# The x^T of batch 1's last head pair by DMA transpose, with a new set of due times: an attention and feed-forward kernel on one core

## The chip, the cores and the metric

The kernel runs on one core of one Trainium2 chip. The metric is the device time of one execution in microseconds. The time before is the median of 8 runs. The profile is of one more execution; times inside it count from the start of its span.

## What is computed

Sorted attention over 4 batches, 8 heads, 768 tokens, 64 values a head, and then a feed-forward network with a squared ReLU. The essence of the reference:

```python
P = sort_net                                  # (4, 8, 8, 8)
for _ in range(5):
    P = exp(P - max(P, -1)); P /= sum(P, -1); P /= sum(P, -2)
k_sorted, v_sorted = P @ blocks of k, P @ blocks of v      # 8 blocks of 96 tokens
attn = softmax(q_block @ k_sorted_block.T / 8)             # block by block
x = (attn @ v_sorted_block) as (3072 tokens, 512)
h = maximum(x @ w_in, 0)                      # (3072, 2048)
out = h * h @ w_out                           # (3072, 512)
```

## The kernel before

**Units.** Attention is worked through in pairs of heads, written (batch, pair), with pairs 0 to 3 of each of the batches 0 to 3. The feed-forward part takes 384 tokens at a time: U0 to U7, two for a batch. Each has 16 up chunks (`up`, L988: four 128x384 matmuls over the four pairs' rows of xT, one for each kc) and three times four down chunks (`down`, L1023: four 128x512 matmuls). U2.5 is the sixth up chunk of U2; D1.2.3 is the last down chunk of the third token tile of U1. An up chunk takes 0.65 us of TensorE, a down chunk 0.863.

**The steps of a pair**, by the letter that stands in DUES (L21) and in this text:

- N and V (`s_nat`, L743): sorted k and v in their natural layout, two pairs at once, so N(2,1) gives pairs 2 and 3 of batch 2. 16 matmuls on 32x32 tiles (L759), then two evictions from PSUM, one for each pair, by ACT or DVE. V is then written to DRAM and read back in another layout by SP (`v_way`, L783 and L789).
- Z (`s_turn`, L810): k and q of one pair transposed by DMA on SP (L816, L839); DVE then splits q in two (L843, L844).
- S (`s_sc`, L643): the scores, two halves of four matmuls (L657), each followed by two exponentials on ACT (L697).
- A (`s_av`, L857): the two halves of the values (L873, 8 matmuls each), each followed by the normalisation on DVE, a reciprocal (L885) and a product (L886).
- X (`s_xt`, L905): x^T, the pair's 128 rows of the tile xT that the up chunks read. It goes one of two ways. Either TensorE transposes eight 96x128 blocks into PSUM (L928) and ACT or DVE copies them to xT (L935), or SP issues a DMA_TRANSPOSE (L910) that goes from SBUF to SBUF[...]. Before the change the second way is taken for batches 2 and 3, for pairs 0 to 2 of batch 1, and for the second half of pairs 0 to 2 of batch 0.
- T and K do for batch 0 what V and N do later; W builds weights of the sorting (`build_wt`, L477).

S halves, A halves, N and V evictions share two PSUM slots (`p2`, ring r2), taken by turns: a step waits until the step two before it in that ring has been read out.

**The order.** A planner in the kernel (`Plan.run`, L136) writes every engine's order by its own costs before anything runs. On TensorE it merges two queues: the attention steps, in the order of their due times, and the feed-forward chunks. A due time is a number of chunks: the step goes as soon as that many have gone and its inputs are there by the plan. Once written, the order of each engine is fixed, and so is that of the DMA issues on SP and POOL: an engine waits for its next instruction's inputs and does nothing else.

**Loads.** q, k and v of batches 2 and 3 are loaded by POOL, six DMAs of 384 KB for each batch (`load_late`, L1136). They overwrite buffers and would disturb other transfers, so a tiny copy on POOL (`hold`, L1138) waits for x^T of the batch before; for batch 2 it waits for pairs 0 to 2 of batch 1 and not for pair 3 (`HP - (b == 2)`, L1139 and L1142). The loads of batch 2 follow it on POOL at once.

The functions that the change touches:

Of the kernel before, what the change touches and what calls it, by code (L numbers as in the profile page):

```python
# [18 lines left out]


DUES = {  # L21
    (0, "K"): (-133.5, -48.0, -102.0, -78.0),
    (0, "S"): (-77.0, -37.5, -97.5, -40.0),
    (0, "T"): (-99.0, -11.5, -42.0, -63.5),
    (0, "A"): (-64.0, 16.0, -15.0, -31.5),
    (0, "X"): (-7.5, 41.5, -9.5, -18.5),
    (0, "W"): (-100.0,),
    (1, "V"): (20.5, 30.5),
    (1, "Q"): (32.0,),
    (1, "N"): (None, 36.0),  # L30
    (1, "Z"): (None, None, 38.0, 43.5),
    (1, "S"): (32.5, 40.5, 43.5, 50.0),
    (1, "A"): (41.0, 41.5, 48.5, 50.0),
    (1, "X"): (45.0, 41.5, 48.5, 55.0),
    (2, "L"): (58.0,),
    (2, "N"): (75.5, 70.5),
    (2, "V"): (63.0, 88.5),
    (2, "Z"): (84.0, 84.5, 90.5, 96.0),
    (2, "S"): (90.0, 96.5, 100.5, 102.0),
    (2, "A"): (95.0, 98.0, 104.0, 102.5),  # L40
    (2, "X"): (100.0, 101.5, 110.0, 104.0),
    (3, "L"): (110.5,),
    (3, "N"): (130.0, 137.5),
    (3, "V"): (117.0, 140.5),
    (3, "Z"): (134.5, 143.0, 154.5, 154.0),
    (3, "S"): (145.0, 150.5, 159.0, 155.0),
    (3, "A"): (148.0, 153.5, 162.5, 156.5),
    (3, "X"): (159.0, 248.0, 167.0, 326.0),
}


# [133 lines left out]
def kernel(  # L185
# [12 lines left out]
    B, H, S, D = q.shape  # L198
# [5 lines left out]
    HP = H // 2  # L204
# [35 lines left out]
    def cost_b(n):  # L240
        return (0.17 + 0.82e-3 * n, 0.15 + 0.53e-3 * n)

    def one_of(eng, cost, fn, deps):
        return plan.add(eng, cost if eng == AD else cost[AD.index(eng)], fn, deps)

    def copy(eng, out, in_):
        if eng == "ACT":
            nc.scalar.copy(out=out, in_=in_)  # L248
        else:
            nc.vector.tensor_copy(out=out, in_=in_)  # L250
# [653 lines left out]

    def s_xt(u, due=0, eng=AD, own=True):  # L905
        early = u.b == 0 and u.halves == (1,) and u.hp < HP - 1
        if early or u.b > 1 or u.b == 1 and u.hp < HP - 1:
            def turn(e):
                t0 = S * u.b + BLK * u.i0
                nc.sync.dma_start_transpose(  # L910
                    out=xT[:, u.hp, t0:t0 + BLK * u.ni].rearrange("p (n q) -> p n q", q=BLK),
                    in_=u.ao.rearrange("p n e d -> p (n e d)"))

            sp = plan.add("SP", 1.4, turn, u.norms)
            op = plan.add("WAY", 6.0 if early else 1.3, lambda e: None, [sp], tail=5.0 if early else None)
            rao.use(u.nao, op)
            for hf in u.halves:
                x_done[u.b, u.hp, hf] = op
            return
        st = {}  # L920

        ring = r1 if own else rf

        def mm(e):
            st["p"] = xtp = ((ps1 if own else psf)
                             .tile([128, u.ni, BLK], BF16, tag="p1" if own else "pf", name="xtp"))
            for n in range(u.ni):
                nc.tensor.transpose(  # L928
                    out=xtp[:, n, :],
                    in_=u.ao[:, n, :, :].rearrange("p e d -> p (e d)"),  # L930
                    identity=ident[0:96, 0:96])

        def ev(e):
            t0 = S * u.b + BLK * u.i0
            copy(e, xT[:, u.hp, t0:t0 + BLK * u.ni], st["p"].rearrange("p n q -> p (n q)"))  # L935

        s1, old = ring.take()
        pe = plan.add("PE", 0.342 if u.full else 0.17, mm, u.norms + old, due)
        op = one_of(eng, cost_b(BLK * u.ni), ev, [pe])
        ring.use(s1, pe, op)  # L940
        rao.use(u.nao, pe)
        for hf in u.halves:
            x_done[u.b, u.hp, hf] = op
# [138 lines left out]
    for name in FIRST.split():  # L1082
        stage, n = name[0], int(name[1])
        eng = "ACT" if stage.isupper() else "DVE"
        stage = stage.upper()
        if stage == "F":
            f_piece(n)
            continue
        if n not in us:
            us[n] = Unit(0, n, (0,))  # L1090
            us[n].q_op = qops[n]
        u = us[n]
        own = (name[2:] == "'") ^ (stage in "TX")
        if stage == "K":
            u.k_op = s_sort(u, 1, early=True, eng=eng, own=own)
        elif stage == "V":
            u.v_op = s_sort(u, 2, early=True, eng=eng, own=own)
        elif stage == "S":
            s_sc(u)
        elif stage == "T":  # L1100
            s_vt(u, eng=eng, own=own)
        elif stage == "A":
            s_av(u)
        else:
            s_xt(u, eng=eng, own=own)
# [6 lines left out]
              "T": lambda b, hp, due: s_vt(units[b, hp], due),  # L1112
              "A": lambda b, hp, due: s_av(units[b, hp], due),
              "X": lambda b, hp, due: s_xt(units[b, hp], due),
              "V": lambda b, g, due: s_nat(b, g, 2, due),
              "N": lambda b, g, due: s_nat(b, g, 1, due)}
# [83 lines left out]
```

The softmax here doesn't subtract the row's maximum and nothing guards it: scores larger than these inputs give would overflow.

## Time and profile before

| | us |
|---|---|
| median of 8 runs (218.43 to 218.96) | 218.66 |
| the profiled execution, its own time | 218.67 |
| its span, first to last instruction | 216.9 |
| TensorE busy | 211.4 |
| ACT busy | 120.5 |
| DVE busy | 110.0 |
| POOL busy | 30.4 |
| TensorE on up chunks (L997) | 87.8 |
| TensorE on down chunks (L1027) | 85.1 |
| X(1,3) on TensorE (L928, 8 transposes, at 74.66) | 0.34 |
| X(1,3)'s copy on DVE (L250) | 0.56 |

The time around the span (1.8 us) is the execution's time less its span. A line of the chain of work that ended last gives start, duration and what; there, a matmul's piece runs from end to end. A line of the timeline gives start, duration, engine, line, operation, output<-inputs and count, and in brackets the engine's idle time before it and what ended that. The DMA view names queue q0 for what POOL issues (software_dynamic) and q1 for what SP issues (hardware_dynamic), with packets, MB and the time that the packets took as a share of 16 engines.

### The profile page before, as it was taken

What the parts mean: (1) busy time and instruction counts of PE and PEld (TensorE: products, weight loads), DVE (VectorE), ACT (ScalarE), POOL (GpSimd) and SP (SyncE); (2) the same over time, 40 slices, a digit from 0 to 9 for tenths busy, and PEclk for the clock granted to TensorE, in tenths of its full rate; (3) what the DMA queues carried; (4) which work ended last, traced back from release to release, by engine and by line L of the source; (5) the groups of instructions that cost most, each with busy time, mean ns of one, the idle gap of its engine ahead of it and who ended that gap; (6) DMA issues with size and microseconds to landing.
All of it is one profiled execution on the core that took longest, in us unless ns stands there. A gap on an engine that the chain in (4) does not pass through costs nothing.

```text
span 216.9 us, 4928 instructions
## 1 busy us (share of the span) xinstructions
PE 211.4 (97%) x1958; PEld 120.0 (55%) x1958; DVE 110.0 (51%) x310; ACT 120.5 (56%) x246; POOL 30.4 (14%) x55
## 2 busy tenths in 40 slices
PE   8989999999999999999999999999999999999994
PEld 3566666446566565446675465446666465456543
DVE  6778748218785446505886055327676155005400
ACT  4665795227955277417884277238765276137521
POOL 7994222200000600000000420000000000000000
DMA  5999999999993599199982699559997310120012
GB/s 64 198 202 207 207 207 205 190 184 260 229 188 99 126 199 216 34 185 209 245 156 74 127 189 215 111 139 126 257 181 144 92 51 0 48 80 20 0 48 97
DMA packets 47831, 31.51 MB, mean 145 GB/s; under 512 B 27264, under 2 KB 42880, under 8 KB 47808
## 3 DMA queue, kind: packets, MB, share of 16 engines
q0 software_dynamic: 12736, 13.63, 39.1%
q1 hardware_dynamic: 35072, 17.56, 36.6%
q8 instruction: 15, 0.25, 0.4%
q14 instruction: 8, 0.07, 0.1%
HBM read 29.70 MB, written 8.72 MB: 177 GB/s over the span
## 4 chain that ended last, share of the span: by engine, by line
PE 91%; DVE 5%; ACT 1%; DMA 1%; issue 1%; DVEq 0%
PE hp L997 39%; PE op L1027 37%; PE p L873 4%; PE p L657 3%; PE p L759 2%; PE op L1055 2%; PE p L667 1%; PE vbp L723 1%; DVE p_sb L402 1%; PE p L624 1%; DMA p_sb<-in_sort_net_dram 1%; PE xtp L928 1%; DVE cs L400 1%; ACT p_sb L432 1%; DVE ao L886 1%
## 5 line engine op out<-in xcount | busy, mean ns | idle before, releaser
L997 PE MATMUL hp<-xT,w_in_bf 128*128 128x384 bf16 x506 | 87.8, 327 | 0.0
L1027 PE MATMUL op<-w_out_bf,h 128*128 128x512 bf16 x368 | 85.1, 379 | 0.0
L1008 DVE TENSOR_TENSOR h<-h 128x384 bf16<-128x384 bf16 x128 | 43.9, 355 | 57.3 <-ACT h L1005 56.9
L1005 ACT ACTIVATE h<-hp 128x384 bf16<-128x384 f32 x128 | 61.9, 494 | 18.2 <-PE hp L997 15.6
L997 PEld LDWEIGHTS <-w_in_bf 128*128 128x128 bf16 x506 | 47.7, 98 | 31.4 <-issue 0.9
L1027 PEld LDWEIGHTS <-h 128*128 128x128 bf16 x368 | 34.3, 98 | 37.0 <-issue 1.0
L248 ACT COPY ob<-op 128x512 f32<-128x512 f32 (+2 forms) x25 | 14.2, 568 | 51.6 <-PE op L1027 49.1
L886 DVE TENSOR_TENSOR ao<-p,rec 96x512 bf16<-96x512 f32 x32 | 22.0, 686 | 1.1
L697 ACT ACTIVATE et<-p 96x384 bf16<-96x384 f32 x40 | 16.8, 487 | 8.0 <-PE p L657 7.7
L873 PEld LDWEIGHTS <-et 96*128 96x128 bf16 x256 | 11.6, 97 | 5.0 <-issue 0.7
L885 DVE RECIPROCAL rec<-p 96x8 f32<-96x8 f32 x32 | 6.4, 200 | 10.5 <-PE p L873 8.7
L1139 POOL COPY held<-xT 1x3 bf16<-1x3 bf16 (+1 forms) x2 | 0.4, 182 | 78.6 <-DMA xT<-ao 78.6
L418 PE MATMUL p<-ones 128*128 128x512 bf16 (+1 forms) x30 | 9.4, 434 | 1.1 <-DVE ones L269 1.1
L657 PEld LDWEIGHTS <-kx 128*128 128x128 bf16 x80 | 8.4, 144 | 2.3 <-issue 0.2
L873 PE MATMUL p<-vblk,et 96*128 96x65 bf16 x192 | 9.5, 193 | 0.0
L657 PE MATMUL p<-qz,kx 128*128 128x192 bf16 x80 | 9.0, 246 | 0.0
L250 DVE CAST kn<-p 128x768 bf16<-128x768 f32 x5 | 4.8, 958 | 8.3 <-PE p L759 8.1
L250 DVE CAST vn<-p 128x768 bf16<-128x768 f32 x6 | 5.7, 956 | 5.8 <-PE p L759 4.4
L322 POOL DMA_DIRECT2D kb<-in_k_dram x10 | 6.4, 642 | 4.4 <-DMA w_in_bf<-in_moe_w_in_dram 2.0
L322 POOL DMA_DIRECT2D qb<-in_q_dram x8 | 6.2, 770 | 5.1 <-DMA w_in_bf<-in_moe_w_in_dram 2.2
L322 POOL DMA_DIRECT2D vb<-in_v_dram x10 | 6.3, 629 | 3.4 <-DMA w_in_bf<-in_moe_w_in_dram 3.4
L687 ACT ACTIVATE et<-p 96x768 bf16<-96x768 f32 x8 | 6.2, 803 | 0.3 <-PE p L667 0.2
(84 smaller groups left out, 123.1 us busy)
## 6 DMA issues: line engine op xcount, KB each, us to landing
out_dram<-ob SPq DMA_DIRECT2D x23, 256.0 KB, 2.3
qb<-in_q_dram POOLq DMA_DIRECT2D x8, 384.0 KB, 11.4
v_way<-vn SPq DMA_DIRECT2D x6, 396.0 KB, 5.3
vblk<-v_way SPq DMA_DIRECT2D x6, 396.0 KB, 4.2
vb<-in_v_dram POOLq DMA_DIRECT2D x6, 384.0 KB, 11.8
kb<-in_k_dram POOLq DMA_DIRECT2D x6, 384.0 KB, 10.8
w_in_bf<-in_moe_w_in_dram POOLq DMA_DIRECT2D x4, 512.0 KB, 11.8
w_out_bf<-in_moe_w_out_dram POOLq DMA_DIRECT2D x4, 512.0 KB, 17.8
```

Source lines behind the costliest of these rows:

```text
L248: nc.scalar.copy(out=out, in_=in_)
L250: nc.vector.tensor_copy(out=out, in_=in_)
L322: nc.gpsimd.dma_start(out=dst, in_=src)
L418: nc.tensor.matmul(out=p2[slot][:, 0, 0:128 * r].rearrange("p (r x) -> p r x", r=r), lhsT=ones, rhs=ones[:, None, :].to_broadcast([128, r, ...
L657: nc.tensor.matmul(out=scp[:, n // 2, 2 * BLK * (n % 2):2 * BLK * (n % 2 + 1)], lhsT=kx_r[u.kx][:, i::NB], rhs=qz_r[u.qz][:, :, :, C0 * i: ...
L697: nc.scalar.activation(out=et.rearrange("p h x -> p (h x)")[:, HS * h:HS * (h + 1)] .rearrange("p (m c a) -> p m c a", c=C0, a=NA), in_=st ...
L873: nc.tensor.matmul(out=oup[:, h, 66 * n:66 * n + D + 1], lhsT=(et_r[u.et[hf]].rearrange("p h x -> p (h x)") [:, BLK * (2 * n + h):BLK * (2 ...
L886: nc.vector.tensor_tensor(out=u.ao[:, n0:n0 + NQ, :, :].rearrange("p n e d -> p e n d"), in0=ov[:, :, :, 0:D], in1=rec[:, :, :, None].to_b ...
L997: nc.tensor.matmul(out=t["hp", nt][:, 0:HS], lhsT=w_in_bf[:, kc, 128 * nt:128 * (nt + 1)], rhs=xT[:, kc, t0:t0 + HS], start=(kc == 0), sto ...
L1005: nc.scalar.activation(out=t["h1", nt], in_=t["hp", nt][:, 0:HS], func=AF.Relu)
L1008: nc.vector.tensor_tensor(out=t["h2"][:, nt, :], in0=t["h1", nt], in1=t["h1", nt], op=ALU.mult)
L1027: nc.tensor.matmul(out=t["op", mt], lhsT=t["h2"][:, nt, 128 * mt:128 * (mt + 1)], rhs=w_out_bf[:, nt, :], start=(nt == 0), stop=(nt == NT ...
```

## The change

The condition in `s_xt` now sends X(1,3) by DMA too, so that all of batch 1 goes that way; the transposes of (1,3) on TensorE and their copy are gone. All due times are new. `hold` and `load_late` stay as they are.

```diff
 DUES = {
...
-    (1, "Z"): (None, None, 38.0, 43.5),
-    (1, "S"): (32.5, 40.5, 43.5, 50.0),
-    (1, "A"): (41.0, 41.5, 48.5, 50.0),
-    (1, "X"): (45.0, 41.5, 48.5, 55.0),
-    (2, "L"): (58.0,),
-    (2, "N"): (75.5, 70.5),
+    (1, "Z"): (None, None, 38.5, 46.5),
+    (1, "S"): (32.0, 39.0, 43.0, 49.0),
+    (1, "A"): (39.0, 42.0, 48.0, 49.0),
+    (1, "X"): (39.5, 56.0, 56.5, 61.5),
+    (2, "L"): (57.0,),
+    (2, "N"): (71.5, 85.0),
...
-    (3, "L"): (110.5,),
-    (3, "N"): (130.0, 137.5),
-    (3, "V"): (117.0, 140.5),
-    (3, "Z"): (134.5, 143.0, 154.5, 154.0),
-    (3, "S"): (145.0, 150.5, 159.0, 155.0),
-    (3, "A"): (148.0, 153.5, 162.5, 156.5),
+    (3, "L"): (132.5,),
+    (3, "N"): (140.0, 142.5),
+    (3, "V"): (136.0, 145.5),
+    (3, "Z"): (144.0, 149.0, 153.0, 152.5),
+    (3, "S"): (145.5, 150.0, 160.0, 153.0),
+    (3, "A"): (147.0, 152.0, 161.0, 159.0),
...
     def s_xt(u, due=0, eng=AD, own=True):
         early = u.b == 0 and u.halves == (1,) and u.hp < HP - 1
-        if early or u.b > 1 or u.b == 1 and u.hp < HP - 1:
+        if early or u.b > 0:
             def turn(e):
                 t0 = S * u.b + BLK * u.i0
                 nc.sync.dma_start_transpose(
```

What this makes of the order on TensorE, outside the first 48 us (before on the left):

```
S(1,3): D1.1.0 D1.1.1 S S D1.1.2 A D1.1.3 A     D1.1.0 S D1.1.1 S A D1.1.2 A D1.1.3
X(1,3): D1.2.2 X D1.2.3 U2.0                    D1.2.2 D1.2.3 U2.0
N(2,*): D2.0.2 N(2,1) D2.0.3 N(2,0) D2.1.0      U2.14 N(2,0) U2.15 ... U3.0 N(2,1) U3.1
batch 2, late pairs: S(2,2) first               S(2,3) first
V(3,0): U4.15 V D4.0.0                          D4.1.3 V D4.2.0
N(3,0): D4.0.1 N D4.0.2                         D4.2.3 N U5.0
N(3,1): D4.2.0 N D4.2.1                         U5.1 N U5.2
V(3,1): D4.2.3 V U5.0                           U5.4 V U5.5
S(3,1): U5.15 S S D5.0.0 A D5.0.1 A S(3,3)      S S U5.15 D5.0.0 A A D5.0.1 S(3,3)
```

On SP one DMA_TRANSPOSE is added behind that of X(1,2), ahead of the output of D1.1; two of batch 3's q transfers go ahead of its first k transfer. The order on POOL is the same.

More of the change, by code (lines that the diff above doesn't have):

```diff
@@ L21 @@
 DUES = {
[L22 to L28, printed above, removed]
+    (0, "K"): (-126.5, -57.5, -110.5, -64.0),
+    (0, "S"): (-79.0, -5.5, -80.5, -56.5),
+    (0, "T"): (-106.0, -26.0, -38.5, -60.0),
+    (0, "A"): (-68.0, 12.5, -11.0, -26.5),
+    (0, "X"): (4.5, 35.0, -10.0, 8.5),
+    (0, "W"): (-85.5,),
+    (1, "V"): (17.0, 29.0),
     (1, "Q"): (32.0,),
     (1, "N"): (None, 36.0),
-    (1, "Z"): (None, None, 38.0, 43.5),
-    (1, "S"): (32.5, 40.5, 43.5, 50.0),
-    (1, "A"): (41.0, 41.5, 48.5, 50.0),
-    (1, "X"): (45.0, 41.5, 48.5, 55.0),
-    (2, "L"): (58.0,),
-    (2, "N"): (75.5, 70.5),
[L37 to L41, printed above, removed]
-    (3, "L"): (110.5,),
-    (3, "N"): (130.0, 137.5),
-    (3, "V"): (117.0, 140.5),
-    (3, "Z"): (134.5, 143.0, 154.5, 154.0),
-    (3, "S"): (145.0, 150.5, 159.0, 155.0),
-    (3, "A"): (148.0, 153.5, 162.5, 156.5),
-    (3, "X"): (159.0, 248.0, 167.0, 326.0),
+    (1, "Z"): (None, None, 38.5, 46.5),
[4 more added lines that the diff above has]
+    (2, "N"): (71.5, 85.0),
+    (2, "V"): (61.0, 88.0),
+    (2, "Z"): (84.0, 85.5, 98.0, 96.0),
+    (2, "S"): (89.5, 96.0, 102.0, 99.0),
+    (2, "A"): (95.5, 97.5, 102.5, 103.0),
+    (2, "X"): (98.0, 126.0, 103.0, 106.0),
+    (3, "L"): (132.5,),
[4 more added lines that the diff above has]
+    (3, "A"): (147.0, 152.0, 161.0, 159.0),
+    (3, "X"): (159.5, 272.0, 165.0, 363.5),
 }
```

## The prediction

> **What bounds the kernel now.** I read the page first (busy times), then the chain that ended last, then the timeline around the change, then the DMA queues by window.
>
> ```profile
> PE 211.4 (97%) x1958; PEld 120.0 (55%) x1958; DVE 110.0 (51%) x310; ACT 120.5 (56%) x246; POOL 30.4 (14%) x55
> ```
>
> TensorE is busy for 211.4 of 216.9 us, so PE work and PE waits are what counts. The chain (start, us, what; PE nearly throughout) shows both:
>
> ```profile
> 74.66 0.34 PE xtp L928 x8
> ...
> 89.27 0.31 PE p L759 x16
> ...
> 90.55 0.53 PE p L759 x16
> ...
> 159.66 0.40 PE p L873 x8
> ...
> 161.18 0.47 PE p L657 x4
> ```
>
> The first line is what the change removes. The others show short waits: an N or V pair (L759 x16) takes 0.31, but 0.53 where it follows another after one chunk; an A half (L873 x8) takes 0.25 elsewhere, here 0.40; an S half (L657 x4) 0.33, here 0.47. From 172 us to the end there is no excess.
>
> The timeline around the removed step:
>
> ```profile
> 69.09 1.21 SPq L910 DMA_TRANSPOSE xT<-ao  x1
> ...
> 71.65 0.41 PE L873 MATMUL p<-vblk,et 96*128 96x65 bf16 x8
> ...
> 72.04 0.18 POOL L1139 COPY held<-xT 1x3 bf16<-1x3 bf16 x1 [32.69 <-DMA xT<-ao]
> ...
> 72.41 0.69 DVE L886 TENSOR_TENSOR ao<-p,rec 96x512 bf16<-96x512 f32 x1
> ...
> 72.52 0.54 POOL L322 DMA_DIRECT2D kb<-in_k_dram  x1 [0.29 <-issue]
> ...
> 75.70 2.60 PE L997 MATMUL hp<-xT,w_in_bf 128*128 128x384 bf16 x15
> ```
>
> X(1,2) is issued at 69.09, has landed when the hold copy runs at 72.04, and that releases batch 2's loads at 72.52. A(1,3)'s second half starts at 71.65 and its normalisation ends at 73.10, 1.45 later. U2 starts at 75.70.
>
> A transfer of this kind has two prices. In 28 to 42 us, with loads running (first fence), and in 61 to 74 us, without (second):
>
> ```profile
> L910 SPq DMA_TRANSPOSE xT<-ao x3: 1181/1181/1274, 29.4 to 38.9; - x3
> ...
> DMA to landing us min/median/max: 7.5/8.3/8.6
> ```
>
> ```profile
> L910 SPq DMA_TRANSPOSE xT<-ao x3: 1212/1213/1215, 62.9 to 69.1; - x3
> ...
> DMA to landing us min/median/max: 2.8/2.9/4.5
> ```
>
> The packet counts of both queues in 34 to 35.5 us say why:
>
> ```profile
> q0 software_dynamic: 233, 0.23, 91.4%
> q1 hardware_dynamic: 233, 0.06, 29.8%
> ```
>
> One packet of the transfer (256 B) goes for one of a load (1 KB)[...].
>
> [...] Here 8 up matmuls take 1.41 right behind a V pair (at 49.41 in the chain) and 1.30 at 32.20[...]; the number of N and V pairs stays the same and each stands alone, so I count no difference.
>
> **The change, step by step.** The program's order says: 8 transposes with their weight loads leave PE, one DMA_TRANSPOSE more on SP, the order of POOL the same, no PE work added.
>
> 1. X(1,3) leaves PE: -0.34 us (first line of the chain). It lay between two down chunks, fully on the path. Its 128x768 copy on DVE (0.56) goes; DVE was idle 1.94 us before it, worth nothing.
>
> 2. N(2,0) moves from one chunk behind N(2,1) to two up chunks behind V(2,0), N(2,1) to one chunk into U3. Two chunks are 1.3 us, and the evictions of a pair take 0.80 (ACT) and 0.96 (DVE): the slot is free, so -0.22 (0.53-0.31). Bounds: 0 to -0.22.
>
> 3. S(3,1) goes ahead of U5.15, and both halves of A(3,1) ahead of D5.0.1. A(3,1) waited 0.15 for its exponentials and S(3,3) 0.14 for the normalisation; with a chunk more between them both fit: -0.29. S(3,2)'s 0.16 (waits for the split of q on DVE, same order) stays.
>
> 4. S(1,3)'s first half goes one down chunk earlier. Its slot is freed by A(1,2)'s first normalisation, 67.54+0.69=68.23; PE would be there at 68.15. +0.13 with the signal.
>
> 5. V(3,0), N(3,0), N(3,1), V(3,1) go later by 4 to 10 chunks. The loads of batch 3 have landed by 138.7, their order on SP puts two q transfers first, and A(3,0) comes about 13 us after V(3,0). S(3,0)'s second half needs the slot of V(3,1), evicted on DVE behind a split of 0.88 us: 0 to +0.15, I take +0.08. Batch 2's pairs 2 and 3 change names only.
>
> 6. The first 48 us: the same instructions, T, S, A of batch 0's second half in another order among U0's chunks. I walked PE, ACT and DVE through it with the durations of before; A(0,1) comes out at 37.6, as now. 0, bounds -0.2 to +0.2.
>
> 7. The new transfer X(1,3). PE from D1.1.0 (67.29): to 68.28 with step 4, then S 0.33, down 0.86, S 0.33, A 0.25, down 0.86: A's second half starts at 70.92. Normalised 1.45 later, 72.37; SP is free, so issued at 72.40. PE goes on: A 0.25 and five downs of 0.863: U2 at 75.49, and its fourth matmul, the first that reads this part of xT, at 75.98 (3 x 0.163 later). On a quiet queue it lands at 72.40+2.85=75.25: 0.73 to spare. But POOL still waits for pairs 0 to 2 only, so the loads are issued at 72.52 as now. X(1,2)'s 800 packets (50 an engine) ran from 1.16 to 2.34 us after issue: here to 74.74. The loads' first packet now comes at 74.14, 14 of them by 74.75. The tail meets them. Loads at full rate:
>
> ```profile
> q0 software_dynamic: 57, 0.18, 106.2%
> ```
>
> These are packets in 75 to 76 us: 16/57=0.28 us each on an engine, plus 0.02 for the short one: 0.30 for each packet still to go. Bounds: none left (the queue already filled goes first, as the output's packets did, which ended at 74.17 just as the loads began): no wait. Or 28 left on the engine that a load reaches at 74.14 (355 of X(1,2)'s 800 were through at the same age): 8.4 us, landing 83.0, wait 7.0. I take 74.4, where 592 of 800 are through: 208/16=13 left, 3.9 us, last packet 78.3, landing 0.5 later, 78.8. Wait 78.8-75.98=+2.8. PE's order is fixed, so nothing fills it; behind U2's first chunk stands everything else.
>
> **The sum** against the profiled execution, 218.67 (span 216.9 and 1.8 around it; the median of the 8 runs is 218.66): -0.34-0.22-0.29+0.13+0.08=-0.64, that is 218.03 without the wait. With it 220.8.
>
> **Rivals.**
> - The transfer is through before the loads reach the engines. For: in the profile the loads' first packets waited for the output's to end, and its own span ends at 74.74, close to their start. Against: one for one in 34 to 35.5. Gives 218.0, faster: the other side. It decides where at most 2 packets an engine are left: 0.73 spare / 0.30.
> - A small overlap, 4 to 6 packets left: wait 0.5 to 1.1, which eats the gain: 218.5 to 219.1, centre 218.7.
> - Batch 3's k and v come late to S(3,0) and A(3,0) (step 5). For: N(3,0)'s transfer starts some 4 us ahead of its use, and transfers beside a v_way write took up to 5.7. Against: by then that write has landed. One late landing by 1 us, with no wait at U2: 219.0.
>
> **Chances.** Overlap that costs over a us (forecast): 0.58. No wait: 0.28. Small overlap: 0.10. Late batch 3: 0.04. A measurement of this kernel tells some 0.2% (0.44 us) from no change: faster below 218.22, slower above 219.10. Faster 0.28, same 0.12, slower 0.60. The range goes from 217.8 (no wait, step 6 at its better end) to 224.2, which takes in waits up to 6.2; the rest of the upper bound (7.0, or more if the loads come sooner) is left out with about 0.1. The forecast's own range is 219.1 to 224.2.
>
> **What would show it.** Right: X(1,3)'s time to landing well over 3 us; a hole in PE before the fourth up matmul of U2, released by DMA xT<-ao; one for one packets on both queues from 74.2. Wrong: landing near 2.9 and no hole. Step 1: no xtp line at 74. Step 2: all N pairs at 0.31. Step 3: A(3,1) at 0.25 and S(3,3) at 0.33. Step 5: no excess at S(3,0) and A(3,0). What would upset it most is another issue time of X(1,3): 0.3 us earlier and the tail is clear of the loads, 0.3 later and half of it is not.

## The result, and the profile after

The changed kernel takes 223.06 us (median of 11 runs, 221.21 to 229.56); the kernel before takes 218.65 in the 31 runs beside it. The ratio of the two is 1.018, with a 95% interval of 1.0161 to 1.0200: slower, by 4.4 us. Single runs lie apart from the rest, 229.56 here (at a mean clock of 0.978) and 6 of the 97 of the kernel before beside the experiments (223.25 to 224.66, at 0.984 to 0.992), and the ratios leave them out. Forecast were 220.8 and a range from 217.8 to 224.2.

The other ten runs fall into two groups. Three take 221.21, 221.26 and 221.49, at a mean granted TensorE clock of 1.000. Seven take 222.86 to 224.14, six of them at a clock of 0.992 and one, 222.97, at 1.000 (a twelfth execution on record, 223.45 at 0.992, is not in the median). The profiled execution is the one of 221.49, so it shows 2.82 us more than the 218.67 of before; the other 1.7 us of the median it does not show.

The row of the page that answers to the forecast hole, before (first) and in the changed kernel (second):

```profile
L997 PE MATMUL hp<-xT,w_in_bf 128*128 128x384 bf16 x506 | 87.8, 327 | 0.0
```

```profile
L997 PE MATMUL hp<-xT,w_in_bf 128*128 128x384 bf16 x506 | 88.6, 327 | 2.8 <-DMA xT<-ao 2.8
```

The last column is idle time ahead of the up matmuls and what ended it. The timeline of the changed kernel around U2, TensorE's lines:

```profile
75.58 0.65 PE L997 MATMUL hp<-xT,w_in_bf 128*128 128x384 bf16 x3
79.03 0.65 PE L997 MATMUL hp<-xT,w_in_bf 128*128 128x384 bf16 x3 [2.80 <-DMA xT<-ao]
```

U2 does its first three matmuls at 75.58 and then stands still until 79.03: the fourth needs X(1,3). The chain that ended last, lines that answer to those shown of before:

```profile
68.34 0.53 PE p L657 x4
...
72.48 6.51 DMA xT<-ao
...
87.16 0.31 PE p L759 x16
...
88.87 0.31 PE p L759 x16
...
162.21 0.50 PE p L873 x16
...
163.58 0.46 PE p L657 x4
```

The transfer, issued at 72.48, takes 6.51 us to its landing at 78.99. The V and N pairs of batch 2 take 0.31 each, where the second of two took 0.53. A(3,1)'s halves take 0.50 together, where one of them alone took 0.40. S(3,3)'s first half still takes 0.46 instead of 0.33, and S(1,3)'s first half, at 68.34, takes 0.53.

From the starts of the first up matmuls in both traces, and the ends (differences are of unrounded times):

| us from the start of the span | before | after | difference | added since the row above |
|---|---|---|---|---|
| U2 starts | 75.70 | 75.58 | -0.12 | -0.12 |
| U4 starts | 123.90 | 126.51 | +2.62 | +2.74 |
| U6 starts | 172.33 | 174.72 | +2.39 | -0.23 |
| TensorE ends | 214.05 | 216.44 | +2.39 | 0 |
| span ends | 216.87 | 219.69 | +2.82 | +0.43 |

U2's first 52 up matmuls take 11.506 instead of 8.543, so the hole is 2.96. The rest of +2.74 is -0.22, the N wait. Two entries are left that the prediction did not have: 0.43 us after TensorE's end, and the 1.7 us of most runs.

### The profile page after: what moved, and what is told of

It is laid out like the page before. It is cut to its first block, busy times and chain, and to the rows that moved or that the text cites. A ratio compares the mean times of both kernels' runs of the same rounds, so it can differ in the third digit from the quotient of the medians.

```text
span 219.7 us, 4913 instructions
## 1 busy us (share of the span) xinstructions
PE 211.6 (96%) x1950; PEld 119.6 (54%) x1950; DVE 108.1 (49%) x308; ACT 120.2 (55%) x247; POOL 30.4 (14%) x55
## 4 chain that ended last, share of the span: by engine, by line
PE 88%; DVE 5%; DMA 4%; ACT 1%; issue 1%; DVEq 0%
PE hp L997 38%; PE op L1027 34%; PE p L873 4%; PE p L657 3%; DMA xT<-ao 3%; PE op L1055 2%; PE p L759 2%; PE p L667 1%; PE vbp L723 1%; DVE p_sb L402 1%; DVE ao L886 1%; PE p L624 1%; DMA p_sb<-in_sort_net_dram 1%; DVE cs L400 1%; ACT p_sb L432 1%
## 5 line engine op out<-in xcount | busy, mean ns | idle before, releaser
L997 PE MATMUL hp<-xT,w_in_bf 128*128 128x384 bf16 x506 | 88.6, 327 | 2.8 <-DMA xT<-ao 2.8
L418 PE MATMUL p<-ones 128*128 128x512 bf16 (+1 forms) x30 | 10.3, 468 | 1.1 <-DVE ones L269 1.1
```

The lines of the kernel that those rows point to most:

```text
L418: nc.tensor.matmul(out=p2[slot][:, 0, 0:128 * r].rearrange("p (r x) -> p r x", r=r), lhsT=ones, rhs=ones[:, None, :].to_broadcast([128, r, ...
L997: nc.tensor.matmul(out=t["hp", nt][:, 0:HS], lhsT=w_in_bf[:, kc, 128 * nt:128 * (nt + 1)], rhs=xT[:, kc, t0:t0 + HS], start=(kc == 0), sto ...
```

## The experiments

**Theory.** Batch 2's loads, issued 0.02 us after X(1,3), keep it from landing; the hole at U2 is the loss, and the hole then costs clock. **Rivals.** The transfer is late by itself at this place; the new due times lose the time; the lower clock has nothing to do with the hole.

### The loads wait for the transfer

```diff
-            nc.gpsimd.tensor_copy(out=held[0:1, 0:HP - (b == 2), b:b + 1],
-                                  in_=xT[0:1, 0:HP - (b == 2), S * b - 1:S * b])
+            nc.gpsimd.tensor_copy(out=held[0:1, 0:HP, b:b + 1],
+                                  in_=xT[0:1, 0:HP, S * b - 1:S * b])
```

> The changed kernel, but POOL's hold ahead of batch 2's loads reads all four pairs of xT, so that the loads are issued when X(1,3) has landed; the order on PE, ACT, DVE and SP is the same. Theory (loads that get ahead of the transfer cost the 2.8 us): X(1,3) lands some 2.85 us after its issue at 72.5, PE has no hole at U2, the loads are issued near 75.4 and land up to 93, still ahead of their use; 218.0 us (217.7 to 218.4), clock 1.000 in all runs. Rival (a transposing transfer is late by itself here, or the late loads make PE wait later at V(2,*) and N(2,*)): over 219.

Measured: 218.69, against 218.95 of before on that chip (ratio 0.9986, interval 0.9967 to 1.0006). X(1,3) lands 2.81 after its issue; U2's 52 matmuls take 8.543, as in the kernel before; from U2's start to the end of TensorE it is 2.96 shorter than in the changed kernel, the length of the hole. The loads land up to 92.3 and nobody waits for them. The transfer is not late by itself. But the forecast of 218.0 was missed by 0.7, and the gain of 0.64 is not there: 0.43 stands after TensorE's end (below). The profiled execution, 219.50, also reached U2 at 76.58, a microsecond late, 0.8 of it lost before D0 began (37.39 instead of 36.60) to a wait of 0.89 for a weight load at 20.2, where both kernels have the same instructions.

### The transfer alone

The kernel before with the new condition and its old due times:

```diff
-        if early or u.b > 1 or u.b == 1 and u.hp < HP - 1:
+        if early or u.b > 0:
```

> The kernel before with its own due times, and only X(1,3) given to the transposing transfer. A(1,3)'s second half stands one down chunk later than in the changed kernel, so the transfer is issued near 73.2, some 0.7 us behind the loads' first issue. Theory: it is again held behind the loads' packets, landing 79.5 to 81; PE would be at U2's fourth matmul at 75.85, a wait of 3.6 to 5.1; 222.0 to 223.5 in runs at full clock. Rival (the due times set the loss): 218.3 to 219.

Measured: 230.03 (ratio 1.0503, 1.0465 to 1.0542), far over the expectation; the loss does not need the new due times. The transfer, issued at 73.36, 0.64 after the first load, needs 12.23 us, of which 3.9 pass before its first packet (1.2 for X(1,2) before the change):

```profile
L997 PE MATMUL hp<-xT,w_in_bf 128*128 128x384 bf16 x506 | 90.8, 333 | 9.4 <-DMA xT<-ao 9.4
```

The DMA view of 79 to 84 us of this kernel, packets, MB and share by queue:

```profile
q0 software_dynamic: 669, 0.78, 92.5%
q1 hardware_dynamic: 670, 0.17, 28.7%
```

One for one in these 5 us. All six runs are at a clock of 0.978 or 0.985, and the matmuls after the hole are slower (90.8 us for the same 506, and 88.6 in the changed kernel), so the 11 us are not the hole of 9.4 alone.

### The due times alone

The changed kernel with the old condition, and X(1,3) due ahead of V(2,0):

```diff
-    (1, "X"): (39.5, 56.0, 56.5, 61.5),
+    (1, "X"): (39.5, 56.0, 56.5, 60.5),
...
-        if early or u.b > 0:
+        if early or u.b > 1 or u.b == 1 and u.hp < HP - 1:
```

> The changed kernel's due times with X(1,3) on PE as before (its own due 60.5 instead of 61.5, so that it stays ahead of V(2,0)); V(2,0) stands one up chunk earlier. Theory (the due times work as forecast, the loss is the transfer's alone): U2 starts 0.34 later than in the changed kernel, no hole, the gains of the N and A waits stay: 218.65 - 0.13 + 0.34 - 0.21 - 0.23 = 218.4 (218.2 to 218.7), clock 1.000. Rival (the due times cost something of their own): 219 or more.

Measured: 219.27, before 218.91 (ratio 1.002, 1.000 to 1.004): a miss by 0.85. The edit is no clean half. X(1,3)'s transposes now stand directly ahead of U2, and its fourth matmul waits for the copy:

```profile
PE hp L997 <- DVE xT L250: 0.2, 1, 0.2
```

Some 0.6 more goes in batch 2 (U2's start to U4's start 48.77, and 47.98 in the changed kernel less its hole); 0.35 of it are two waits of S (0.85 instead of 0.66 at 102.74, 0.49 instead of 0.33 at 113.08), and the rest stays open. These due times do not pay without the transfer. Still, no such loss as 4.4 comes from them.

### The loads a little later

```diff
+            for _ in range(3 if b == 2 else 1):
-            nc.gpsimd.tensor_copy(
+                nc.gpsimd.tensor_copy(
```

> The changed kernel with POOL's hold copied 3 times for batch 2, so that batch 2's loads are issued some 0.4 us later, near 72.9, and their first packets come near 74.15. Prediction's picture (the transfer runs at its quiet pace until then and only its tail alternates): packets of X(1,3) from 73.65 at quiet pace, some 350 through by 74.15, the rest one for one with loads, landing 77.5 to 79.5, a hole of 1.5 to 3.5. Rival (the transfer escapes as soon as its first packets are ahead): landing near 75.4, no hole, 218.5.

> The same with 7 copies: loads issued some 1.1 us later, near 73.6, first packets near 74.85, when the transfer's 800 packets are through at its quiet pace (2.34 us after issue, 74.82). Theory: landing near 75.4, no hole or under 0.3, 218.3 to 218.8. Rival (only waiting for the landing helps): landing over 77, a hole over 1.

Each was executed once. The edit shown is the first; the second has 7 copies instead of 3. From the transfer's issue to the first load's it is 0.02 us in the changed kernel, 0.29 in the first and 1.26 in the second. In the second, the DMA view of 73.5 to 75 us holds the whole transfer and no load:

```profile
q1 hardware_dynamic: 800, 0.20, 69.1%
```

It lands 2.79 after its issue, the hole is gone, the run takes 218.54. With 3 copies, 630 of the 800 packets are through by 75.0, when the loads' first come (at 74.97; the forecast had some 350 through at 74.15). What is left meets the loads in 75 to 77 us, where the 134 of SP's queue leave 36 of the transfer for later:

```profile
q0 software_dynamic: 79, 0.24, 91.2%
q1 hardware_dynamic: 134, 0.03, 9.9%
```

The transfer lands 7.75 us after its issue, later than in the changed kernel and than forecast (80.55, forecast 77.5 to 79.5): 224.65, with this row:

```profile
L997 PE MATMUL hp<-xT,w_in_bf 128*128 128x384 bf16 x506 | 90.3, 330 | 4.0 <-DMA xT<-ao 4.0
```

Being a quarter of a microsecond better off was no help in this execution; the transfer that was wholly through ahead of the loads was safe.

### The hole without the transfer, and the transfer's delay without the hole

First, the changed kernel with TensorE kept at work:

```diff
+                for _ in range(18 if (g, nt) == (2, 0) else 0):
+                    nc.tensor.matmul(
+                        out=t["hp", nt][:, 0:HS], lhsT=w_in_bf[:, 0, 0:128],
+                        rhs=xT[:, 0, t0:t0 + HS], start=True, stop=True)
                 for kc in kcs:
```

> The changed kernel with 18 more matmuls 128x384 (18 x 0.163 = 2.9 us) ahead of U2's first chunk, into the PSUM bank that the chunk then overwrites: PE works through the wait instead of standing idle. The time at full clock should stay at 221.3 to 221.7. Theory A (the idle hole is what brings the clock of 0.992 in most runs of the changed kernel and 1.7 us more): all runs at clock 1.000, median 221.5. Theory B (the clock falls for another reason, the chip or the DMA traffic): most runs again at 0.992, median about 223.2.

Second and third, the kernel before with its copy of X(1,3) made longer, 7 and then 13 times:

```diff
-            copy(e, xT[:, u.hp, t0:t0 + BLK * u.ni], st["p"].rearrange("p n q -> p (n q)"))
+            for _ in range(7 if (u.b, u.hp) == (1, HP - 1) else 1):
+                copy(e, xT[:, u.hp, t0:t0 + BLK * u.ni], st["p"].rearrange("p n q -> p (n q)"))
```

> The kernel before, with X(1,3) still on PE, but its copy from PSUM on DVE done 7 times over (6 x 0.558 = 3.35 us more), so that U2's fourth matmul waits for DVE and not for a transfer: about 3.35 - 0.75 = 2.6 us of hole in PE at the same place, with no transfer and no change of due times. At full clock 221.2. Theory A (the hole brings the lower clock): most runs at 0.992, median near 223. Theory B (the clock has to do with the transfer or the due times): all runs at 1.000 and 221.2.

> The kernel before with X(1,3) on PE and its copy done 13 times: a hole of about 2.9 + 6 x 0.558 = 6.2 us, no transfer in it. Theory[...]: every run at a clock under 1.000 (0.992 or 0.985)[...]: 218.65 + 6.2 + 1 to 2.6 = 226 to 227.5. Rival (the clock falls by chance): some runs at 1.000 and 224.9.

| kernel | idle at U2 | median | runs, and their clock |
|---|---|---|---|
| changed | 2.8, DMA | 223.06 | three, 221.21 to 221.49, at 1.000; seven, 222.86 to 224.14, at 0.992 (one at 1.000); 229.56 at 0.978 |
| filled | 0 | 221.73 | five, 221.42 to 222.08, at 0.998 to 1.000; 228.70 at 0.985 |
| copy 7 times | 2.8, DVE | 222.00 | four, 221.43 to 222.03, at 1.000; 223.97 and 225.49 at 0.992 |
| copy 13 times | 6.4, DVE | 227.89 | four, 226.86 to 228.32, all at 0.985 |

With TensorE at work through the same delay, no run has the second group's time. The hole of the same length made by DVE did not do what theory A said: four of six runs stay at full clock, and two lower ones do not tell much where the kernel before, with no hole there, has such runs too. With the longer hole all four have more of it, and take a little more than the 226 to 227.5 forecast, in which 1 to 2.6 us for the lower clock were the author's estimate. The last kernel's table by window (PE, PEld, DVE, ACT, POOL busy, then the granted clock, DMA share and GB/s) shows what happens:

```profile
78.00:80.00 2.00, 0.00 (x0) 0.00 (x0) 1.88 (x4) 0.00 (x0) 0.00 (x0) 0.82 1.06 152
80.00:82.00 2.00, 0.00 (x0) 0.00 (x0) 1.90 (x4) 0.00 (x0) 0.00 (x0) 0.50 1.22 256
82.00:84.00 2.00, 1.23 (x4) 0.56 (x4) 0.81 (x3) 0.49 (x1) 0.00 (x0) 0.50 1.10 220
84.00:86.00 2.00, 2.00 (x8) 0.99 (x7) 0.59 (x2) 0.58 (x2) 0.00 (x0) 0.50 1.09 204
86.00:88.00 2.00, 2.00 (x14) 1.19 (x13) 0.84 (x3) 1.38 (x4) 0.00 (x0) 0.98 1.03 159
```

In the hole the clock falls to half and stays there after work has begun again: 8 matmuls in two microseconds instead of 14. From the 0.82 and the 0.98, half clock lasts from 79.28 to 86.08, 6.8 us. The kernel with loads 0.4 later, whose hole is 4.0, has one such stretch:

```profile
80.00:82.00 2.00, 1.41 (x5) 0.71 (x5) 0.31 (x1) 0.49 (x1) 0.00 (x0) 0.62 1.09 270
82.00:84.00 2.00, 2.00 (x9) 0.92 (x7) 0.40 (x2) 0.77 (x2) 0.00 (x0) 0.52 1.26 240
```

from 80.48 to 83.92, 3.4 us. In the transfer alone, whose hole is 9.4, the clock is 0.81 in 80 to 82 us, 0.50 from there to 91 and 0.76 in 91 to 92: half clock from 81.24 to 91.48, 10.24 us. After holes of 4.0, 6.4 and 9.4 us half clock thus lasts 3.4, 6.8 and 10.2, and the mean clocks of the three profiled executions are 0.992, 0.985 and 0.978. In the profiles of the changed kernel and of the copy done 7 times, each with a hole of 2.8, the mean clock is 1.000. What decides whether a hole of 2.8 us is followed by half clock was not shown.

By an estimate from the stretch behind the hole of 4.0, 3.4 us at half clock are worth 3.4 / 2 = 1.7 us of work and bring the mean clock of 221 us to 1 - 0.5 x 3.4 / 221 = 0.992: both are what the second group shows. So that a hole in TensorE can bring half clock is shown. That it brings the 0.992 of the changed kernel (six of ten runs) is argued from this: no profile caught a run of that group, and the changed kernel was not measured again beside the filled one, in the same session and on the same chip. A longer hole in those runs, where the transfer lands later, stays a rival; the run of 222.97 is as long at a clock of 1.000.

### The end after TensorE

The waits on SP in the last microseconds of the kernel before (first) and the changed one (second): line, what it waited for, us in total, times, the longest.

```profile
SPq L1195 <- DMA out_dram<-ob: 0.8, 2, 0.4
```

```profile
SPq L1195 <- DMA out_dram<-ob: 1.2, 1, 1.2
```

At the end SP checks the semaphores of all engines and of eight DMA lanes (a lane is the semaphore that a transfer of SP signals when it lands), in a fixed order, one check every 62 ns or so: in the changed kernel those of the eight lanes pass from 218.37 to 218.81. The transfers of SP take the eight lanes by turns; the changed kernel's last two signal the eighth and the first. Before, the last output signals the last of them, and the checks ahead of it pass while it is under way. One transfer more moves it to the first of the eight: SP waits there for 1.2 us and does the seven other checks afterwards, 7 x 0.062 = 0.43. The kernel before with one transfer more, and the changed kernel with the hold on four pairs and seven more:

```diff
-        sp = plan.add("SP", 0.55, lambda e: nc.sync.dma_start(out=dst, in_=st["ob"][:, 0:n]), [op])
+        def send(e):
+            w = 128 // parts
+            for r in range(0, 128, w):
+                nc.sync.dma_start(out=dst[r:r + w, :], in_=st["ob"][r:r + w, 0:n])
+
+        sp = plan.add("SP", 0.55, send, [op])
```

with `parts` 2 for the last tile of D6 in the first, and 4, 4 and 2 for D6's three tiles in the second.

> The kernel before with one output transfer of D6 cut into two halves: one transfer more on SP's queue, nothing else. Theory: the last output's semaphore moves from the last to the second place in the row of checks at the end, seven checks of some 62 ns then come after its landing: the end after PE goes from 2.85 to 3.26, 218.65 + 0.42 = 219.1. Rival (the transfer of xT itself brings the longer end): 2.85 and 218.65.

> The changed kernel with the hold on all four pairs (as in e1_hold_four), and D6's three output transfers cut into 4, 4 and 2 parts, seven transfers more on SP's queue at a time when it is quiet. The number of SP's transfers decides which of the eight semaphores the last output signals, and so its place in the row of checks at the kernel's end. Theory: PE ends at 213.5 after the span's start (before: 214.05), and the end after PE is 2.85 as before instead of 3.26; 218.65 - 0.57 = 218.1. Rival (the end after PE depends on something else in the changed kernel): 3.26 again, 218.5.

Measured: 219.33 against 218.69 (ratio 1.0028, 1.0013 to 1.0044), 0.2 over the forecast of 219.1, and 218.08 against 218.69 (0.9965, 0.9953 to 0.9977), as forecast. The time from TensorE's end to the span's end is 3.25 in the first and 2.83 in the second. Over all twelve traces it is 2.82 to 2.84 where the number of transfers is that of the kernel before or seven more than the change's, and 3.25 to 3.27 where it is one more. The second kernel is the fastest of all, 0.6 us faster than the kernel before. Its row has no hole, and its wait at the end is back:

```profile
L1002 PE MATMUL hp<-xT,w_in_bf 128*128 128x384 bf16 x506 | 88.5, 327 | 0.0
```

```profile
SPq L1200 <- DMA out_dram<-ob: 0.8, 2, 0.4
```

## Why the prediction was right, and where not

**Step 1** (X(1,3) leaves TensorE, -0.34) and **step 4** (S(1,3) waits for its slot, +0.13): U2 starts 0.12 earlier; forecast was 0.21. The wait of step 4 is 0.21 instead of 0.13: S at 68.34 takes 0.53, 0.20 over the usual 0.33, and starts 0.02 late.

**Step 2** (N(2,0)'s slot wait, -0.22): as forecast, 0.31 for each pair.

**Steps 3 and 5** (-0.29 and +0.08): the stretch from U4 to U6 is 0.23 shorter, by the sum -0.21. That the two agree is luck, for the terms were off both ways: A(3,1)'s wait is gone (-0.15), S(3,3)'s stays (0.46, -0.01), and S(3,0)'s two halves, which were to lose 0.08, take 0.67 where they took 0.75 (-0.08).

**Step 6** (first 48 us, 0): D0's first chunk starts at 36.60 in both profiled executions.

**Step 7** (wait of 2.8): the wait is 2.96, the issue at 72.48 (forecast 72.40), the landing at 78.99 (78.8). Yet the picture behind it, "The tail meets them", was wrong: 592 packets were to be through before the loads came. The DMA view of the changed kernel in 73.5 to 74.5 us has no packet of SP's queue:

```profile
q0 software_dynamic: 18, 0.06, 67.5%
```

The loads were there first, at 73.77, and the whole transfer met them: its first packet came only at 74.70, 2.2 after its issue, where X(1,2)'s came after 1.2. Before, the loads' first packet came 1.62 after their issue, when the output of D1.1, issued by SP at 72.46, was just ending. The change puts X(1,3) ahead of that output on SP, the output is issued at 73.79, and the loads come 1.27 after issue. That the output's packets make the difference is argued, but the twelve traces agree: 1.25 to 1.27 where SP has no packets under way, 1.57 to 1.89 where it has, and 1.37 where they have just ended. The step named the output's packets and did not ask where they would be once the transfer stood before them. In 74.5 to 76.25 us (first) it goes nearly one for one, and in 76.25 to 77.5 (second) most of the rest goes at once:

```profile
q0 software_dynamic: 93, 0.29, 93.8%
q1 hardware_dynamic: 81, 0.02, 8.9%
```

```profile
q1 hardware_dynamic: 521, 0.13, 86.8%
q0 software_dynamic: 33, 0.05, 24.7%
```

Of the first load's 128 packets 111 have begun by 76.25, the last ends at 77.3, and the second load's first comes at 77.6. That gap let the transfer out, not a count of 13 packets at 0.30: it is by luck that the landing, 78.99, is so near to the forecast 78.8. Where the loads have no gap, the same transfer takes 12.23 (the transfer alone). With loads 0.4 later, under 70 packets, some four for each engine, were left at 75.25, which at 0.30 would be 1.3 us; it landed 5.3 after that. By the sizes in the trace, the last of its 768 packets of 256 B ended at 77.07; the other 32, of 4 B, went from 77.9 to 80.3, where those of X(1,2) before, on a quiet queue, went from 71.20 to 71.43, beside the last of its 256 B packets (71.41). So "0.3 us earlier and the tail is clear" was wrong as well: against the loads this transfer was issued 0.27 earlier than in the changed kernel, and 1.24 earlier was enough.

**The sum.** Without the wait, TensorE's end moves by -0.12 - 0.22 - 0.23 = -0.57, forecast -0.64. With the wait of 2.96 and the 0.43 at the end this is +2.82, which is exactly 221.49 - 218.67. **Two terms were missing**: the end after TensorE (+0.43), for which the number of SP's transfers would have had to be counted against the eight lanes; and the 1.7 of most runs, 3.4 us at half clock if the argument above holds, which the forecast did not price. With them the sum is 218.66 + 2.82 + 1.7 = 223.2, and the median 223.06.

**The rivals.** "Through before the loads" is what the kernels with the hold on four pairs and with loads 1.1 later are. Their 218.69 and 218.54 miss the 218.0 of that rival by 0.7 and 0.5, of which the end is 0.43; with the lanes put right it is 218.08. "A small overlap" of 4 to 6 packets, priced at a wait of 0.5 to 1.1, is what the kernel with loads 0.4 later came to at 75.25: its hole is 4.0. Late loads for batch 3 did not show.

**Open.** What parts the runs of the changed kernel: six of ten show 0.992, and two of six with a hole of the same length made by DVE. The run of 222.97, which is as long at a mean clock of 1.000. Why the transfer's first packets come late beside loads, and its last ones later still.

## What to carry to other kernels

Before a short-packet transfer is put beside bulk loads, ask which packets are first at the engines, and let the loads wait for its landing if TensorE does: here that costs nothing and removes 2.96 us. Price a hole in TensorE with the half clock behind it: here 3.4 us of it followed a hole of 4.0, and with a hole of 2.8 made by DVE two runs of six had a clock of 0.992 and four 1.000. And when the number of transfers changes, look at the checks at the kernel's end: here one transfer more or fewer is worth 0.43 us.

## What the runs showed of the hardware

- A transposing transfer of 800 packets (768 of 256 B, 32 of 4 B) takes 2.8 us on quiet queues (2.81 with the hold on four pairs, 2.79 with loads 1.1 later), 6.5 where the loads have a gap, 7.75 with only a fifth of it left when they come (one execution), and 12.2 against loads without a gap.
- The first packets of a load can be slow: in the changed kernel 18 of them had 67.5% of 16 engines for 1 us, 0.6 us each, where later ones (93 in 1.75 us, 93.8%) take 0.28. Over the twelve traces the mean of the first 16 goes from 0.28 to 0.81 us.
- A TensorE hole of 4.0 us was followed by half clock for 3.4 us (mean clock 0.992), one of 6.4 by 6.8 us (0.985 in all four runs), one of 9.4 by 10.2 (0.978); two profiled holes of 2.8 by none (mean clock 1.000).
- A check of a semaphore that is already there takes SP some 62 ns, and seven of them in a row at the kernel's end (218.37 to 218.81 in the changed kernel, 0.43 us) are seen in its time.
